# The last six layers of the first block in three passes, and where their weight splits stand in a step

## The chip, the cores and the metric

The kernel runs on one core of one Trainium2 chip. A core has engines that work side by side, each through a queue of its own in order: TensorE (PE, matrix products), VectorE (DVE, elementwise, reads PSUM), ScalarE (ACT, elementwise and copies, reads PSUM), GpSimd (POOL, elementwise on SBUF alone) and SyncE (SP, which here issues the DMA transfers). The metric is the device time of one execution in microseconds, as the median of several runs.

## The reference, cut to what matters

A linear-attention layer with decay (state `S x D x D` per head) makes `x` of 3072 tokens by 384. Then two feed-forward layers follow; the change is in the first one's weights and products:

```
def _moe_ref(x, w_in, w_out):          # 3072 x 384, 384 x 2048, 2048 x 384
    h = x @ w_in
    relu6 = np.clip(h + 3.0, 0.0, 6.0)
    g = h * relu6 / 6.0
    return (g @ w_out).astype(np.float32)
```

All of it is in 32-bit floating point.

## The kernel before, in words

The tokens are worked in six blocks `c` of 512 (128 steps of time for each of 4 batch entries). The hidden width 2048 is worked in 16 slices `f` of 128. In a *step* `n`, one pair (block, slice) is taken: `ff1` makes `hps`, the 128x512 product of the slice's input weights with the block's `x` in PSUM; ACT (line 462) and DVE (line 463, called *stt* below) apply the activation to it; and `ff2` adds the product of an earlier step's result with the slice's output weights onto `o`, two steps late (`while len(todo) > 2`). The first block is special: its slices 0 to 4 are done in halves of 256 tokens (steps 0 to 9), and from step 10 on it is whole slices, `n = f + 5`, up to step 20. The second block is steps 21 to 36, `n = f + 21`.

A product is done in one of two ways. *Full 32-bit*: three products of 128x128 by 128x512 (`emit_h_f32`, line 451, and `emit_out_f32`, line 457; each appears as two matmul records). *Three passes* (`emit_h`, line 445, and `emit_out`, line 474): both factors are split into a rounded high part and the low rest, and nine products are summed. Three passes need the parts of the weights, of `x` and of the activation's result `g`. In the first block the slices below `F32_F` (12) are done in full 32-bit, the rest, and all later blocks, in three passes.

The weights arrive as 64-bit numbers. For a slice `f` the class `Weight` does `load` (DMA into `raw`), `scale` (ACT, line 146), `bits` (DVE, lines 151 and 152; its result `x`, a staging tile with three buffers, is sent by a DMA into the slice's place in `wide_a` or `wide_b`, line 155), and later `parts`: ACT copies the high part (line 161) and DVE subtracts it from the value to leave the low part (line 162).

Between the products the attention runs as *jobs* `j` (one per batch entry and block), of which jobs 4 to 7 belong to the second block and 8 to 11 to the third. `plan(j, n)` puts a job over steps n to n+5: `scans` (DVE, line 280) and `bonus1` (POOL, lines 307, 308) in step n; `muls` (DVE, 303), `bonus2` (DVE, 312) and `decay` (POOL, 295 to 298) in n+1; `fill` (ACT, 338) in n+2, and in the middle of that step `pe_a` (PE, 357), `choose` (DVE, 363) and `copy_kt` (ACT, 350); in n+3 `pe_y` (PE, 393 and 399), `pe_u`, `copy_y` (ACT, 405, then seven transfers by SP that lay the result out) and `add_u` (DVE, 381); in n+5 `split` (ACT 421, POOL 422), which makes the parts of the next block's `x`. Jobs 7, 8, 9 and 10 begin at steps 15, 19, 23 and 27.

The order on every engine is written by hand. A step emits the list `before[n]`, then `ff1`, then `between[n]`, then `ff2` of two steps ago, then `behind[n]`; `pin()` ties each engine's instructions to this order:

```
        run(before[n])
...
        ff1(c, f, cols)
        run(between[n])
        while len(todo) > 2:
            ff2(*todo.pop(0))
        run(behind[n])
        pin()
```

A three-pass `ff1` also issues `emit_split` (ACT line 467, POOL line 468) right after the activation, so `ff1` of such a step is L462, stt, L467, L468. `x_parts` (lines 597 to 601) makes the parts of the first block's own `x`. The PSUM tile that `pe_y` writes is the one that `choose` of the same job has read, since their pool has one buffer; the tiles `hps` have two.

Of the kernel before, what the change touches and what calls it, by code (L numbers as in the profile page):

```python
# [9 lines left out]
F32 = mybir.dt.float32  # L10
# [3 lines left out]
AF = mybir.ActivationFunctionType  # L14
ALU = mybir.AluOpType
# [8 lines left out]
KT = DM // 128  # L24
F1 = 2048 // 128
# [4 lines left out]
WP = 4 * DM  # L30
NG = F2 // 3
LAGS = (5, 0, 0, 0, 0, 0)
F32_F = 12


@with_exitstack
def kernel(
# [15 lines left out]
    nc = tc.nc  # L53
# [23 lines left out]
    x0 = st_p.tile([128, KT, TOK], F32, tag="x0", name="x0", bufs=1)  # L77
# [53 lines left out]

    class Weight:
        def __init__(self, src):
            self.src, self.near = src, False

        def load(self):
            self.raw = st_p.tile([128, 2 * DM], U64, tag="raw", name="raw", bufs=3)
# [11 lines left out]
        def bits(self):  # L149
            x = st_p.tile([128, 2 * DM], U32, tag="x", name="x", bufs=3)  # L150
            nc.vector.tensor_scalar(x, self.words()[0], 29, None, ALU.logical_shift_right)
            nc.vector.scalar_tensor_tensor(
                out=x, in0=self.mag.bitcast(U32), scalar=3, in1=x, op0=ALU.logical_shift_left, op1=ALU.bitwise_or)
            self.x = x.bitcast(F32).rearrange("p (a n) -> p a n", a=2)
            nc.sync.dma_start(
                out=self.dst[:, :, 1, :].bitcast(U32), in_=x.rearrange("p (a n) -> p a n", a=2))
            if not self.near:
                self.x = self.dst[:, :, 1, :].bitcast(F32)
# [103 lines left out]
    xts = {0: xt_p.tile([128, KT, 2, TOK], F32R, tag="xt", name="xt")}  # L262
# [192 lines left out]
    def emit_out_f32(acc, slot, g, first, cols):  # L455
        for m in range(KT):
            nc.tensor.matmul(  # L457
                acc[m][:, cols], slot[:, m * 128:(m + 1) * 128], g,
                start=first, stop=True, skip_group_check=not first)
# [5 lines left out]
    def emit_split(a, n, p=None):  # L465
        g = (p or rg_p).tile([128, 2, n], F32R, tag="g", name="g")
        nc.scalar.activation(out=g[:, 0, :], in_=a, func=AF.Copy)  # L467
        nc.gpsimd.tensor_tensor(out=g[:, 1, :], in0=a, in1=g[:, 0, :].bitcast(F32), op=ALU.subtract)  # L468
        return g
# [9 lines left out]
    def new_acc():  # L479
        return [ps_o.tile([128, TOK], F32, tag=f"o{m}", name=f"o{m}") for m in range(KT)]  # L480
# [51 lines left out]
    wa = [Weight(wa_d[f]) for f in range(F1)]  # L532
# [9 lines left out]
    before, between, behind = ([[] for _ in steps] for _ in range(3))  # L542
# [38 lines left out]
        if f + 3 < F1:  # L581
            behind[n] += [wa[f + 3].load]
    for f in range(F1):
        before[f + 19 if f < F32_F else f + LAGS[0] - 1] += [wa[f].parts]
    behind[2] += [lambda: jobs[4].load("w", "rk", "rks", "v")]
    behind[4] += [lambda: jobs[5].load("w", "rk", "v")]

# [6 lines left out]
    for c in range(1, NC_):  # L594
        norm_plan(c, first[c], False)

    def x_parts():
        for k in range(KT):
            h = xts[0][:, k, 0, :]
            nc.scalar.activation(out=h, in_=x0[:, k, :], func=AF.Copy)  # L600
            nc.vector.tensor_tensor(out=xts[0][:, k, 1, :], in0=x0[:, k, :], in1=h.bitcast(F32), op=ALU.subtract)

    behind[F32_F + LAGS[0] - 2] += [x_parts]
    acc, norms, todo = None, {}, []


# [12 lines left out]
    def ff1(c, f, cols):  # L619
        n = cols.stop - cols.start  # L620
        ps = ps_h.tile([128, n], F32, tag="h", name="hps")
        if c == 0 and f < F32_F:
            if cols.start:
# [4 lines left out]
        else:  # L628
# [3 lines left out]
            g = emit_split(a, n)  # L632
        x = wa[f].x[:, 1] if c == 0 and f < F32_F else wpair[f][:, 1]
        todo.append((c, f, cols, g, x))

    def ff2(c, f, cols, g, x):
        nonlocal acc
        first, last = f == 0 and cols.start == 0, f == F1 - 1
        if first:
            acc = new_acc()  # L640
        if c == 0 and f < F32_F:
            emit_out_f32(acc, x, g, first, cols)
# [5 lines left out]
    def run(fs):  # L648
        for x in fs:
            x()  # L650
# [302 lines left out]
    for i in range(2):  # L953
        nc.sync.dma_start(
            out=uc[64 * i:64 * i + D, :, i], in_=u_d.rearrange("o (p i d) -> i d (o p)", p=NP, i=2)[i])
# [24 lines left out]
    for f in range(W1):  # L980
        wa[f].dst = wpair[f]
        wa[f].near = f < 2
    run((j0.scans, j0.pairs, j0.pe_bonus, j0.muls, j1.pairs, j0.fill, j0.pe_a, wa[0].scale, j1.pe_bonus, j1.fill))
    run((j1.scans, j0.choose, j1.muls, j1.pe_a, j0.pe_y0, wa[0].bits, wa[3].load, j1.choose, j1.pe_y0))
    run((wa[1].scale, wa[1].bits, wa[4].load, j2.pairs, j2.scans, j0.copy_y0, j1.copy_y0))
# [150 lines left out]
    for j in range(6 * NG + 1):  # L1136
        p, k = divmod(j, 2 * NG)
# [142 lines left out]
```

## Time and profile before

| | |
|---|---|
| median of 3 runs | 946.01 us (945.63 to 946.22) |
| the profiled execution | 945.5 us |
| its span in the profile | 943.7 us |
| PE busy | 928.6 us (98%) |
| DVE, ACT, POOL busy | 645.8, 475.8, 534.2 us |
| granted TensorE clock, mean | 0.998 |

The span is what the profiler saw from the first to the last instruction; 1.8 us lie around it. A row of a timeline gives the start, the time from start to end, the engine and line, what is written from what, and in brackets the idle time of the engine before it with what ended that. Merged instructions of one kind carry their count (x9).

### The profile page before, as it was taken

What the parts mean: (1) busy time and instruction counts of PE and PEld (TensorE: products, weight loads), DVE (VectorE), ACT (ScalarE), POOL (GpSimd) and SP (SyncE); (2) the same over time, 40 slices, a digit from 0 to 9 for tenths busy, and PEclk for the clock granted to TensorE, in tenths of its full rate; (3) what the DMA queues carried; (4) which work ended last, traced back from release to release, by engine and by line L of the source; (5) the groups of instructions that cost most, each with busy time, mean ns of one, the idle gap of its engine ahead of it and who ended that gap; (6) DMA issues with size and microseconds to landing.
All of it is one profiled execution on the core that took longest, in us unless ns stands there. A gap on an engine that the chain in (4) does not pass through costs nothing.

```text
span 943.7 us, 14286 instructions
## 1 busy us (share of the span) xinstructions
PE 928.6 (98%) x5085; PEld 734.6 (78%) x5085; DVE 645.8 (68%) x913; ACT 475.8 (50%) x946; POOL 534.2 (57%) x454
## 2 busy tenths in 40 slices
PE   5999999999999999999999999999999999999998
PEld 5875578778878887777888888887877778888886
DVE  7787767777778777776545477648888557554555
ACT  4554556546645554655454653446555444433331
POOL 0043255766756776674466677489466679335423
PEclk9999999999999999999999999999999999999999
DMA  9888532247546555652752387763699742644321
GB/s 347 299 300 286 201 135 84 85 144 251 190 132 202 176 168 154 229 179 59 239 197 97 130 309 265 272 242 156 220 376 335 262 162 89 245 167 153 149 79 67
DMA packets 63127, 184.77 MB, mean 196 GB/s; under 512 B 8912, under 2 KB 23248, under 8 KB 58448
## 3 DMA queue, kind: packets, MB, share of 16 engines
q1 hardware_dynamic: 63056, 183.87, 55.1%
q8 instruction: 40, 0.66, 0.3%
q14 instruction: 31, 0.25, 0.1%
HBM read 134.29 MB, written 39.32 MB: 184 GB/s over the span
## 4 chain that ended last, share of the span: by engine, by line
PE 90%; DVE 3%; DMA 2%; ACT 2%; SPq 1%; issue 1%; POOL 1%; POOLq 0%; DVEq 0%; ACTq 0%
PE o L474 17%; PE hps L445 16%; PE o L757 15%; PE pe L757 10%; PE pc L757 8%; PE pa L757 4%; PE hps L451 4%; PE o L457 3%; PE aps L357 3%; PE pb L757 3%; PE yps L399 2%; PE pd L757 1%; PE yps L393 1%; PE ktp L345 1%; PE yps L434 1%
## 5 line engine op out<-in xcount | busy, mean ns | idle before, releaser
L468 POOL TENSOR_TENSOR g<-a,g 128x512 fp32r<-128x512 f32 x84 | 116.0, 1381 | 146.6 <-ACT g L467 144.5
L463 DVE SCALAR_TENSOR_TENSOR a<-a,hps 128x512 f32<-128x512 f32 x84 | 57.2, 681 | 86.6 <-ACT a L462 85.1
L474 PE MATMUL o<-g,wide_b 128*128 128x512 f32 x441 | 113.3, 399 | 0.0
L445 PE MATMUL hps<-xt,wide_b 128*128 128x512 f32 x441 | 111.9, 398 | 0.0
L757 PE MATMUL o<-xt,wide_b 128*128 128x512 f32 x405 | 107.6, 395 | 0.0
L462 ACT ACTIVATE a<-hps,half 128x512 f32<-128x512 f32 x84 | 57.4, 684 | 92.5 <-PE hps L445 88.0
L445 PEld LDWEIGHTS hps<-xt,wide_b 128*128 128x128 f32 x441 | 82.7, 187 | 21.2 <-issue 1.2
L474 PEld LDWEIGHTS o<-g,wide_b 128*128 128x128 f32 x441 | 81.2, 188 | 19.5 <-issue 0.5
L467 ACT ACTIVATE g<-a 128x512 fp32r<-128x512 f32 x84 | 53.1, 632 | 79.4 <-DVE a L463 77.3
L757 PEld LDWEIGHTS o<-xt,wide_b 128*128 128x128 f32 x405 | 76.0, 188 | 18.2
L474 PE MATMUL o<-g,wide_a 128*128 128x512 f32 x315 | 78.7, 394 | 0.0
L280 DVE TENSOR_TENSOR_SCAN w<-w,dd 128x520 f32<-128x520 f32 x48 | 75.4, 1570 | 4.7 <-DMA w<-in_dram 3.1
L445 PE MATMUL hps<-xt,wide_a 128*128 128x512 f32 x315 | 77.6, 390 | 0.2 <-POOL xt L422 0.2
L445 PEld LDWEIGHTS hps<-xt,wide_a 128*128 128x128 f32 x315 | 59.0, 188 | 13.3 <-POOL xt L422 0.6
L474 PEld LDWEIGHTS o<-g,wide_a 128*128 128x128 f32 x315 | 58.2, 188 | 12.3 <-issue 0.2
L792 DVE TENSOR_TENSOR q<-pc,q 128x512 f32<-128x512 f32 x80 | 55.1, 688 | 17.6 <-PE pc L757 6.7
L338 ACT ACTIVATE a<-iperm,cb 128x128 f32<-128x128 f32 x192 | 58.5, 388 | 0.1
L858 POOL TENSOR_TENSOR q<-q,q 128x512 f32<-128x512 f32 x36 | 49.2, 1366 | 13.6 <-DVE q L792 13.4
L757 PE MATMUL o<-g,wide_b 128*128 128x512 f32 (+1 forms) x216 | 55.4, 390 | 0.0
L854 ACT ACTIVATE q<-q 128x512 f32<-128x512 f32 x40 | 25.3, 633 | 48.5 <-DVE q L792 48.5
L792 DVE TENSOR_TENSOR q<-pe,q 128x512 f32<-128x512 f32 x40 | 27.5, 688 | 32.1 <-PE pe L757 32.1
L307 POOL TENSOR_TENSOR rks<-rks 128x384 f32<-128x384 f32 x20 | 32.3, 1617 | 30.3 <-DMA rks<-in_dram 23.5
(206 smaller groups left out, 2005.2 us busy)
## 6 DMA issues: line engine op xcount, KB each, us to landing
wraw<-in_dram SPq DMA_DIRECT2D x36, 384.0 KB, 4.1
wide_b<-wo SPq DMA_DIRECT2D x12, 1152.0 KB, 8.3
w<-wd SPq DMA_DIRECT2D x10, 1280.0 KB, 6.1
wide_b<-wd SPq DMA_DIRECT2D x10, 1280.0 KB, 6.0
w<-in_dram SPq DMA_DIRECT2D x24, 520.0 KB, 3.9
rk<-in_dram SPq DMA_DIRECT2D x24, 512.0 KB, 5.0
raw<-in_dram SPq DMA_DIRECT2D x16, 768.0 KB, 7.5
rks<-in_dram SPq DMA_DIRECT2D x20, 384.0 KB, 5.7
```

The costliest lines, as they stand in the source:

```text
L280: nc.vector.tensor_tensor_scan(out=x, data0=x, data1=dd.rearrange("p a h j -> p (a h j)"), initial=0.0, op0=ALU.mult, op1=ALU.add)
L338: nc.scalar.activation(out=self.head(h), in_=iperm, func=AF.Copy, scale=self.cb[:, h, :])
L445: nc.tensor.matmul(ps, slot[:, l, k * 128:(k + 1) * 128], xt[:, k, r, :], start=(k == 0 and j == 0), stop=(k == KT - 1 and j == 2))
L451: nc.tensor.matmul(ps, slot[:, k * 128:(k + 1) * 128], xt[:, k, :], start=(k == 0), stop=(k == KT - 1))
L462: nc.scalar.activation(out=a, in_=ps, func=AF.Relu, scale=1.0 / 6.0, bias=half)
L463: nc.vector.scalar_tensor_tensor(out=a, in0=a, scalar=1.0, in1=ps, op0=ALU.min, op1=ALU.mult)
L467: nc.scalar.activation(out=g[:, 0, :], in_=a, func=AF.Copy)
L468: nc.gpsimd.tensor_tensor(out=g[:, 1, :], in0=a, in1=g[:, 0, :].bitcast(F32), op=ALU.subtract)
L474: nc.tensor.matmul(acc[m][:, cols], slot[:, l, m * 128:(m + 1) * 128], g[:, r, :], start=(first and j == 0), stop=(parts or last and j == ...
L757: nc.tensor.matmul(ps, lhs[:, l, :], rhs[:, r, :], start=first and j == 0, stop=True, skip_group_check=not (first and j == 0))
L792: nc.vector.tensor_tensor(out=out, in0=a, in1=b, op=op)
L858: eng.tensor_tensor(out=o, in0=src, in1=self.gate.o[i], op=ALU.mult)
```

## The change: what it does

`F32_F` becomes 10, so that slices 10 and 11 of the first block (steps 15 and 16) are done in three passes, like 12 to 15. For these six slices `bits` no longer sends its result by DMA (`stays`): `parts` reads the staging tile and writes both parts in place. The parts of slices 10 and 11 are made at the end of steps 13 and 14. Those of slices 12 to 15 stay in steps 16 to 19, and move from the end of the list `before` to its head. Those of slices 0 to 9, which the second block uses, stay in steps 19 to 28, and move from `before` to the end of `behind`. `x_parts` is cut in three, at the end of steps 6, 7 and 8 in place of step 15, with the subtraction on POOL in place of DVE.

```
-F32_F = 12
+F32_F = 10
...
-            self.src, self.near = src, False
+            self.src, self.near, self.stays = src, False, False
...
             self.x = x.bitcast(F32).rearrange("p (a n) -> p a n", a=2)
+            if self.stays:
+                return
             nc.sync.dma_start(
...
     for f in range(F1):
-        before[f + 19 if f < F32_F else f + LAGS[0] - 1] += [wa[f].parts]
+        if f < F32_F:
+            behind[f + 19] += [wa[f].parts]
+        else:
+            if f < 12:
+                behind[f + 3] += [wa[f].parts]
+            else:
+                before[f + 4].insert(0, wa[f].parts)
...
-    def x_parts():
-        for k in range(KT):
-            h = xts[0][:, k, 0, :]
-            nc.scalar.activation(out=h, in_=x0[:, k, :], func=AF.Copy)
-            nc.vector.tensor_tensor(out=xts[0][:, k, 1, :], in0=x0[:, k, :], in1=h.bitcast(F32), op=ALU.subtract)
-
-    behind[F32_F + LAGS[0] - 2] += [x_parts]
+    def x_parts(k):
+        h = xts[0][:, k, 0, :]
+        nc.scalar.activation(out=h, in_=x0[:, k, :], func=AF.Copy)
+        nc.gpsimd.tensor_tensor(out=xts[0][:, k, 1, :], in0=x0[:, k, :], in1=h.bitcast(F32), op=ALU.subtract)
+
+    for k in range(KT):
+        behind[6 + k] += [lambda k=k: x_parts(k)]
...
+    for f in range(F32_F, F1):
+        wa[f].stays = True
```

The queues of ACT and DVE in one step of the second block, say step 24 (slice 3, `muls` of job 9, `split` of job 8), are then, with `c` for the copy of a `parts` and `d` for its subtraction (`square` is a copy of the normalisation that follows a block):

```
before: ACT: L462, L467, split 8, square       DVE: muls 9, bonus2 9, d5, stt
        (c5 ahead of L462)
after:  ACT: L462, L467, split 8, c5, square   DVE: muls 9, bonus2 9, stt, d5
```

## Rows read from the trace of the kernel before

**Rows 1.** The page, busy time of PE: us, share of the span, instructions.

```profile
PE 928.6 (98%) x5085; PEld 734.6 (78%) x5085; DVE 645.8 (68%) x913; ACT 475.8 (50%) x946; POOL 534.2 (57%) x454
```

**Rows 2.** Waits of PE: line waited for: total us, times, longest.

```profile
PE yps L393 <- DVE a L363: 0.9, 1, 0.9
PE hps L445 <- POOL xt L422: 0.2, 1, 0.2
```

**Rows 3.** The chain that ended last: start, us, what.

```profile
101.53 2.58 PE hps L451 x6
104.11 2.58 PE o L457 x6
...
132.56 2.10 PE o L474 x9
```

**Rows 4.** Timeline of ACT and SP: the wait for a removed transfer, and its issue.

```profile
113.47 0.85 ACT L161 ACTIVATE wide_b<-wide_b 128x768 fp32r<-128x768 f32 x1 [1.62 <-DMA wide_b<-x]
...
114.43 0.65 SPq L155 DMA_DIRECT2D wide_b<-x  x1
```

**Rows 5.** Timeline of POOL, in steps 9, 18, 19 and 20.

```profile
60.58 1.30 POOL L307 TENSOR_TENSOR rks<-rks 128x384 f32<-128x384 f32 x1 [6.79 <-DVE a L363]
...
118.55 1.94 POOL L307 TENSOR_TENSOR rks<-rks 128x384 f32<-128x384 f32 x1
...
125.42 1.62 POOL L468 TENSOR_TENSOR g<-a,g 128x512 fp32r<-128x512 f32 x1 [3.03 <-ACT g L467]
127.00 1.73 POOL L422 TENSOR_TENSOR xt<-x,xt 128x384 fp32r<-128x384 f32 x1
```

**Rows 6.** Timeline of DVE, steps 14 to 19.

```profile
93.03 1.64 DVE L152 SCALAR_TENSOR_TENSOR x<-mag,x 128x768 uint32<-128x768 uint32 x1
...
96.23 1.24 DVE L280 TENSOR_TENSOR_SCAN w<-w,dd 128x520 f32<-128x520 f32 x1
...
100.34 1.89 DVE L601 TENSOR_TENSOR xt<-x,xt 128x512 fp32r<-128x512 f32 x3 [1.10 <-ACT xt L600]
102.15 1.28 DVE L303 TENSOR_TENSOR rk<-rk,w 128x512 f32<-128x512 f32 x2
...
103.82 0.95 DVE L162 TENSOR_TENSOR wide_b<-wide_b 128x768 fp32r<-128x768 f32 x1
...
117.72 1.96 DVE L280 TENSOR_TENSOR_SCAN w<-w,dd 128x520 f32<-128x520 f32 x1
...
124.00 0.67 DVE L463 SCALAR_TENSOR_TENSOR a<-a,hps 128x512 f32<-128x512 f32 x1
```

**Rows 7.** Timeline of ACT, steps 15 to 20.

```profile
104.73 0.91 ACT L146 ACTIVATE mag<-raw 128x768 f32<-128x768 f32 x1
105.54 2.44 ACT L338 ACTIVATE a<-iperm,cb 128x128 f32<-128x128 f32 x8
...
108.81 0.69 ACT L462 ACTIVATE a<-hps,half 128x512 f32<-128x512 f32 x1
...
117.14 0.58 ACT L405 ACTIVATE y<-yps 128x512 f32<-128x512 f32 x1
117.61 0.83 ACT L161 ACTIVATE wide_a<-wide_a 128x768 fp32r<-128x768 f32 x1
...
124.71 0.63 ACT L467 ACTIVATE g<-a 128x512 fp32r<-128x512 f32 x1 [1.86 <-DVE a L463]
125.25 0.51 ACT L421 ACTIVATE xt<-x 128x384 fp32r<-128x384 f32 x1
```

**Rows 8.** Timeline of PE and DVE: where jobs 9 and 10 meet.

```profile
155.74 1.36 DVE L363 COPY_PREDICATED a<-mask,aps 128x512 f32<-128x512 uint32 x2
...
157.25 0.67 PE L393 MATMUL yps<-rk,st 64*64 64x128 f32 x16
...
177.26 1.34 DVE L363 COPY_PREDICATED a<-mask,aps 128x512 f32<-128x512 uint32 x2
...
178.74 0.67 PE L393 MATMUL yps<-rk,st 64*64 64x128 f32 x16 [0.88 <-DVE a L363]
```

## The prediction

> **What bounds the kernel now.** I read the page first: PE is busy 98% of the span [rows 1]. The waits of PE come next. Past the start-up there are two of weight, 0.2 us for the split of `x` into the second block and 0.9 for a `choose`, both where blocks one and two meet [rows 2]. So PE sets the end, and a change pays what it takes off PE less what PE newly waits for. Then I read the timelines of the queues over the steps that the change touches; there ACT, DVE and POOL hand work to each other in a fixed order, with little to spare. Job 9's `choose` ends at 155.74 + 1.36 = 157.10 and PE's `pe_y` starts at 157.25; job 10's ends at 178.60, and there PE waits 0.88 [rows 8]. A slower ring of these three engines comes straight out as PE time.
>
> **PE's own work.** A product costs 2.58 in full 32-bit and 2.10 in three passes [rows 3]. Slices 10 and 11 have two each: 4 x 0.48 = **-1.92**. The Trainium skill ("FP8 and Floating Point Precision", section TensorE Precision Notes) says that true 32-bit takes four passes; beside three at 2.10 that would be 2.80 and -2.8 in all. The trace has 2.58, and I keep -1.92.
>
> **The transfers taken away.** Six of 393 KB (128 x 768 numbers of 4 bytes), with 0.65 us of SP's queue each [rows 4]. What is freed: the copy of slice 14 waited 1.62 for one [rows 4], and loads behind them on SP go out earlier. PE waited for none of it, so I count 0; a gain through it would have to show in a wait of PE, and rows 2 have only the two that I count below.
>
> **`x_parts` on POOL, steps 6 to 8.** DVE loses 1.89 at step 15 [rows 6]. POOL gets three subtractions of about 1.3 (as 60.58), into the 6.79 us in which it idled before that row [rows 5]; ACT gets three copies of some 0.6 in slack steps. They delay job 4's chain by about 0.6 and job 5's `bonus1` by about 1.4; PE is a step away from both. Between 0 and +0.5; I take 0.
>
> **Two habits of the queues.** An engine starts its next instruction about 0.1 before the shown end of the last (117.14 + 0.58 against 117.61), and another engine takes over some 0.03 after it (124.00 + 0.67 against 124.71) [rows 6, 7]. And DVE and POOL hold each other up: a scan takes 1.24 at 96.23 but 1.96 at 117.72, while POOL's L307 runs 1.94 beside it; the split L422 takes 1.73 at 127.00 beside a subtraction of DVE [rows 5, 6]. The Trainium skill ("SBUF — State Buffer", section SBUF: two separate sides) calls their shared port a lock held for the whole instruction; with no overlap at all of the two, my sum would come out about 0.5 us dearer. The rows, where the one held up finishes about 0.15 sooner than that, decide.
>
> **Steps 14 to 21: the first seam.** I wrote the new order of each queue as a timetable, with the rows' durations, and found this chain through DVE and ACT. From the end of `bits` 13 at 94.6 [rows 6]:
> - DVE: parts 11 is new there, 0.87; both scans of job 7 held up by `bonus1`, 3.8: step 15's stt at 99.2.
> - stt 0.7; ACT's L467, new, 0.54; `copy_y` 0.49; `scale` 0.81; copy of parts 12 0.85 [rows 7]: 102.6. DVE: subtraction 0.87, muls and reduce 1.67 (102.15 to 103.82) [rows 6]: stt of step 16 at 105.15.
> - 0.7; L467 0.54; `scale` 0.81; copy of parts 13, now ahead of `fill`, 0.74; `fill` 2.35; L462 0.7 [rows 7]: stt of step 17 at 111.0.
> - 0.6; `choose` 1.2; `bits` 15 held up by two POOL instructions, 2.8; parts 14 0.87: stt of step 18 at 116.5.
> - 0.7; L467 0.54; `copy_y` 0.49; copy of parts 15 0.86: 119.1. DVE: the subtraction held up, 1.7; scans 1.9, 0.1 and 1.2: stt of step 19 at 124.0.
>
> That is where it stood before (124.00 [rows 6]), although PE is now 1.92 ahead. After it ACT does L467, then the copy of parts 0, now in front of the split of job 7, which runs 126.0 to 126.5 and not at 125.25 [rows 7]. POOL's L422 begins at 126.6, meets the subtraction of parts 0 on DVE and takes 1.7 [rows 5]: it ends at 128.3. Before, it ended at 128.73 and PE waited 0.2 for it [rows 2, 5]; PE now wants it at 128.55 - 1.92 = 126.6. **A wait of 1.7 instead of 0.2.** PE keeps 0.45 of its 2.1.
>
> **Steps 19 to 28: parts at the end of the step.** Before, the copy of a parts was on ACT ahead of L462 and the subtraction on DVE ahead of the stt, mostly with its copy long done. Now the subtraction stands directly behind the stt, and its copy behind L467, which itself waits for that stt: DVE idles (0.68 + 0.03) + 0.54 + 0.86 - 0.60 = 1.5 us in every such step, with `scans` or `muls` of the next queued behind it. And as L467 also releases POOL's L468, the subtraction meets it and takes about 1.3.
>
> PE needs 178.74 - 0.88 - 157.25 = 20.6 us from one `pe_y` to the next [rows 8], eight products of 2.10 and 3.8 of attention, about half of it on each of the two steps that carry it. The ring needs:
> - Job 8. At 127.5 DVE has finished parts 0; muls, held up, and reduce 2.3; stt to L462 of step 21 with copy 1 and `fill` between, 5.05; stt and `choose` 1.9: done at 136.8. PE would be there at 157.25 - 20.6 - 0.45 = 136.2. **Wait 0.6.**
> - Job 9, counted from `pe_y` 8 at 136.8: attention and the block's last product 4.2; two ACT copies of the block's sum and copy 3, 1.9; subtraction and scans 3.3; stt to the subtraction of parts 4, 2.1; it, muls and reduce 3.2; stt, L467, split, copy 5, square, `fill`, L462 6.0; stt and `choose` 1.9. That is 22.6 against 20.6. **Wait 2.0.**
> - Job 10, from `choose` to `choose`: to step 26's stt 1.8; stt, L467, `copy_y`, copy 7 2.6; subtraction and scans, held up by `bonus1`, 5.0; stt to parts 8 2.1; it, muls (held up) and reduce 4.0; stt, L467, split, copy 9, `fill`, L462 5.5; stt and `choose` 1.9. That is 22.8. **Wait 2.2**, in place of 0.88.
>
> From step 29 on no parts are left (before: until step 30), the ring has slack again, and PE keeps the loss to the end.
>
> **Sum.** -1.92 - 0.2 - 0.88 + 1.7 + 0.6 + 2.0 + 2.2 = **+3.5**. The same timetable for the old order ends L422 at 128.4 (row 128.73) and job 10's `choose` at 177.55 (row 178.60): it falls short by up to 1.0 over these steps, and may do so here. I take +4.0: 945.5 + 4.0 = 949.5 for an execution like the profiled one. The median shown is 0.5 above that one, so **950.0**. Bounds: with no new wait at all -3.0 (943.0); with held-up instructions at their longest +5.2, and with the 0.5 of `x_parts` about +5.7 (951.7).
>
> **Rivals.**
> - *Faster: the ring keeps pace.* The parts leave the way of the stt, so that L467 and the split go earlier, and DVE's 1.5 us of idling falls into time that it had to spare (it is busy 645.8 of 943.7 [rows 1]). Its place is steps 19 to 28, its price the same -1.92 and up to -1.1 of old waits: 943.0 to 944.1 after adding 0.5 (with one wait of 1.4 left in job 9, which the timetable still has when no instruction holds up another, 944.4). It decides from where the seam is 1.7 shorter and the cycles 2 us shorter than I count. Against it: scans, muls and splits are plainly held up in rows 5 and 6, and `choose` had 0.15 to spare in job 9 and none in job 10 [rows 8].
> - *About the same: only the seam costs.* The wait of 1.7 comes, the job cycles hold at 20.6: -1.92 - 0.2 - 0.88 + 1.7 = -1.3, 944.7. Or one cycle pays and the sum is near 0. For it: half of each cycle (the steps with `fill` and `pe_y`) has room on DVE.
> - *The change does nothing for PE*, since three passes wait for parts 10 or 11: parts 11 end at 95.4 and are wanted at 101.53 - 0.48 [rows 3], and parts 10 have as much of a step. No chance of weight.
>
> **How the numbers follow.** I give the forecast 0.70, the ring that keeps pace 0.17, the seam alone or one cycle 0.13. 0.2% is 1.9 us, about what a measurement here can tell from no change: faster is under 944.1, slower over 947.9. So faster 0.17, same 0.13, slower 0.70. The forecast's own range is 948.0 to 952.3; the range that reaches to the others is 943.8 to 952.3.
>
> **What would show it.** Three-pass products in steps 15 and 16 at 2.1 each. A wait of PE for L422 of 1 us or more at step 21; then waits of `pe_y` for `choose` in jobs 8, 9 and 10, of which the last two are near 2. DVE idle by about 1.5 in front of L162 in steps 19 to 28, ended by ACT's L161. If L162 stands there with little idle, or PE's waits past step 21 stay under 1 us in sum, the prediction is wrong, and on the fast side.

## The result, and the profile after

| | before | after |
|---|---|---|
| median of 6 runs, us | 946.12 (945.24 to 946.90) | 951.52 (949.34 to 953.98) |
| ratio, 95% interval | | 1.006 (1.0049 to 1.0070) |
| profiled execution, us | 945.5 | 951.95 |
| its span, us | 943.7 | 950.2 |

The change makes the kernel slower by 5.4 us. It was forecast slower, at 950.0 in a range of 943.8 to 952.3. Below `bits` the code of the kernel after stands two lines lower and, from L593 on, eight: L464, L465, L469, L470 are the activation, the stt and the two parts of `emit_split`, L163 and L164 the two halves of a `parts`, L365 is `choose`, L395 the first product of `pe_y`, L424 POOL's split.

Busy time of PE on the page of the kernel after, in us, with its share of the span and its instructions:

```profile
PE 929.4 (98%) x5097; PEld 738.4 (78%) x5097; DVE 645.6 (68%) x910; ACT 476.8 (50%) x948; POOL 543.6 (57%) x459
```

Twelve more PE instructions are there (four products of nine for six), and PE is busier by only 0.8 us than in [rows 1], so 5.7 of the 6.5 us by which the span grew are waiting. Waits of PE in the kernel after (total us, times, longest):

```profile
PE cps L328 <- DVE rp L322: 8.8, 1, 8.8
PE yps L395 <- DVE a L365: 3.6, 3, 2.2
...
PE hps L447 <- POOL xt L424: 1.2, 1, 1.2
PE pe L765 <- DMA w<-wd: 1.1, 1, 1.1
...
PE hps L447 <- DVE wide_a L164: 0.3, 1, 0.3
```

Beside [rows 2], the split wait went from 0.2 to 1.2, the `choose` waits from one of 0.9 to three, and two lines are new: the one for a subtraction of a `parts`, and one for a DMA. Now PE's timeline, where each of them stands:

```profile
88.42 2.74 PE L453 MATMUL hps<-x,wide_b 128*128 128x512 f32 x6
...
127.59 0.39 PE L447 MATMUL hps<-xt,wide_a 128*128 128x512 f32 x1
129.15 2.14 PE L447 MATMUL hps<-xt,wide_a 128*128 128x512 f32 x8 [1.17 <-POOL xt L424]
...
137.74 0.67 PE L395 MATMUL yps<-rk,st 64*64 64x128 f32 x16 [0.60 <-DVE a L365]
...
151.03 1.89 PE L447 MATMUL hps<-xt,wide_a 128*128 128x512 f32 x7 [0.26 <-DVE wide_a L164]
...
160.91 0.67 PE L395 MATMUL yps<-rk,st 64*64 64x128 f32 x16 [2.22 <-DVE a L365]
161.51 1.52 PE L401 MATMUL yps<-a,v 128*64 128x128 f32 x16
...
183.89 0.67 PE L395 MATMUL yps<-rk,st 64*64 64x128 f32 x16 [0.80 <-DVE a L365]
...
707.02 0.94 PE L765 MATMUL pe<-wide_b,w 128*128 128x512 f32 x3 [1.09 <-DMA w<-wd]
```

Three of these rows are anchors: the product of step 14, the first of step 21, and job 10's `pe_y`. In the kernel before the last began at 178.74 [rows 8], the others here:

```profile
87.12 2.74 PE L451 MATMUL hps<-x,wide_b 128*128 128x512 f32 x6
...
128.20 0.39 PE L445 MATMUL hps<-xt,wide_a 128*128 128x512 f32 x1
```

After, the three stand at 88.42, 127.59 and 183.89: +1.30, -0.61, +5.15. So PE gains 1.91 between the first two, and loses 5.76 between the others. The +1.30 arose at start-up, ahead of everything that the change touches (PE's first wait, for `rp`, is 8.8 here and was 7.9 before); among the kernels below the start-up differs from one profiled execution to the next by as much. What the change did by step 31 is **+3.85**.

The row of L401 at 161.51 takes 1.52 where the same row (L399, at 157.85) took 1.09 before. Windows of 3 us there (busy time of each engine, then PE's granted clock, the DMA share and GB/s):

```profile
158.00:161.00 3.00, 0.78 (x8) 0.35 (x10) 1.93 (x3) 2.25 (x5) 0.74 (x1) 1.00 0.00 0
161.00:164.00 3.00, 3.00 (x49) 2.74 (x50) 1.75 (x3) 2.25 (x5) 2.10 (x3) 0.67 0.00 0
164.00:167.00 3.00, 3.00 (x11) 2.41 (x12) 2.08 (x4) 1.62 (x3) 2.55 (x2) 0.76 0.13 38
167.00:170.00 3.00, 3.00 (x15) 2.48 (x14) 2.93 (x3) 0.69 (x1) 2.92 (x3) 1.00 0.10 27
```

PE was busy for 0.78 of the first 3 us, and behind that wait the granted clock fell for a while to the lower of its two levels, 1.2 GHz. The two windows lose 3 x 0.33 + 3 x 0.24 = 1.7 us. This fall belongs to the execution that was profiled: it lists a mean granted clock of 0.996, two of the six timed ones 1.000 (949.34 and 951.08 us), and one such fall alone would take that mean to 0.998 (1.7 us of 950). Against the kernel before, the waits sum to 1.17 - 0.19 + 0.60 + 0.26 + 2.22 + 0.80 - 0.88 = 3.98; with -1.92 for the products and 1.7 for the clock that is 3.76, of the 3.85 seen.

What feeds those waits is seen on DVE (the bracket is idle time ahead, and what ended it):

```profile
126.82 1.43 DVE L164 TENSOR_TENSOR wide_a<-wide_a 128x768 fp32r<-128x768 f32 x1 [1.43 <-ACT wide_a L163]
...
132.73 1.41 DVE L164 TENSOR_TENSOR wide_a<-wide_a 128x768 fp32r<-128x768 f32 x1 [1.43 <-ACT wide_a L163]
...
149.56 1.41 DVE L164 TENSOR_TENSOR wide_a<-wide_a 128x768 fp32r<-128x768 f32 x1 [1.44 <-ACT wide_a L163]
...
155.40 1.02 DVE L164 TENSOR_TENSOR wide_a<-wide_a 128x768 fp32r<-128x768 f32 x1 [1.85 <-ACT wide_a L163]
...
158.83 0.69 DVE L465 SCALAR_TENSOR_TENSOR a<-a,hps 128x512 f32<-128x512 f32 x1 [2.41 <-ACT a L464]
159.44 1.33 DVE L365 COPY_PREDICATED a<-mask,aps 128x512 f32<-128x512 uint32 x2
```

Ten subtractions stand at the end of a step. Each begins after an idle that the copy of the same `parts` ends: 1.37 to 1.85 in seven of them, 0.66 to 0.88 in three. Four run 1.41 to 1.43 where one took 0.95 before [rows 6]; they begin while POOL's L470 of the same step still runs (from 126.13 for 1.30, beside the first). The other six take 0.96 to 1.17. At 158.83 the last two rows show job 9's end of it: the stt waits for ACT's L464, which stands behind `fill` and the copy, and `choose` behind it ends at 160.77, when PE has already been waiting.

### The profile page after: what moved, and what is told of

Its sections match the earlier page's. It is cut to its first block, busy times and chain, and to the rows that moved or that the text cites. A ratio compares the mean times of both kernels' runs of the same rounds, so it can differ in the third digit from the quotient of the medians.

```text
span 950.2 us, 14303 instructions
## 1 busy us (share of the span) xinstructions
PE 929.4 (98%) x5097; PEld 738.4 (78%) x5097; DVE 645.6 (68%) x910; ACT 476.8 (50%) x948; POOL 543.6 (57%) x459
## 4 chain that ended last, share of the span: by engine, by line
PE 83%; DVE 8%; ACT 4%; DMA 3%; issue 3%; SPq 0%; ACTq 0%; DVEq 0%
PE o L476 17%; PE hps L447 15%; PE o L765 13%; PE pe L765 9%; PE pc L765 8%; PE pa L765 4%; PE hps L453 3%; PE pb L765 3%; PE aps L359 2%; PE o L459 2%; PE yps L401 2%; DVE w L282 1%; PE pd L765 1%; PE yps L395 1%; PE yps L436 1%
## 5 line engine op out<-in xcount | busy, mean ns | idle before, releaser
L470 POOL TENSOR_TENSOR g<-a,g 128x512 fp32r<-128x512 f32 x86 | 116.9, 1359 | 144.7 <-ACT g L469 144.6
L465 DVE SCALAR_TENSOR_TENSOR a<-a,hps 128x512 f32<-128x512 f32 x86 | 58.6, 681 | 93.1 <-ACT a L464 91.5
L476 PE MATMUL o<-g,wide_b 128*128 128x512 f32 x459 | 118.0, 400 | 0.0
L447 PE MATMUL hps<-xt,wide_b 128*128 128x512 f32 x459 | 116.5, 397 | 0.0
L464 ACT ACTIVATE a<-hps,half 128x512 f32<-128x512 f32 x86 | 58.8, 684 | 96.6 <-PE hps L447 93.2
L447 PEld LDWEIGHTS hps<-xt,wide_b 128*128 128x128 f32 x459 | 86.1, 187 | 22.0 <-issue 1.0
L476 PEld LDWEIGHTS o<-g,wide_b 128*128 128x128 f32 x459 | 84.4, 188 | 20.2 <-issue 0.5
L469 ACT ACTIVATE g<-a 128x512 fp32r<-128x512 f32 x86 | 54.4, 633 | 89.3 <-DVE a L465 87.2
L765 PEld LDWEIGHTS o<-g,wide_b 128*128 128x128 f32 x216 | 40.0, 188 | 9.4
```

What stands on the lines that cost most here:

```text
L447: nc.tensor.matmul(ps, slot[:, l, k * 128:(k + 1) * 128], xt[:, k, r, :], start=(k == 0 and j == 0), stop=(k == KT - 1 and j == 2))
L464: nc.scalar.activation(out=a, in_=ps, func=AF.Relu, scale=1.0 / 6.0, bias=half)
L465: nc.vector.scalar_tensor_tensor(out=a, in0=a, scalar=1.0, in1=ps, op0=ALU.min, op1=ALU.mult)
L476: nc.tensor.matmul(acc[m][:, cols], slot[:, l, m * 128:(m + 1) * 128], g[:, r, :], start=(first and j == 0), stop=(parts or last and j == ...
L765: nc.tensor.matmul(ps, lhs[:, l, :], rhs[:, r, :], start=first and j == 0, stop=True, skip_group_check=not (first and j == 0))
```

## The experiments

All times are medians in us; ratios are to the kernel before, timed beside each on the same chip.

**One half alone, and the other half alone.** e1 is the kernel before with nothing but the `parts` of slices 0 to 11 at the end of their steps; e2 the kernel after with those of 0 to 9 back ahead.

```
e1 (on before):  before[f + 19] -> behind[f + 19]   for f < F32_F
e2 (on after):   behind[f + 19] -> before[f + 19]   for f < F32_F
```

> The kernel before, with one edit: the parts of slices 0 to 11 stand at the end of steps 19 to 30 and no longer ahead of the product. My theory (DVE idles behind the activation until ACT has done L467 and the copy): no wait at step 21, since parts 0 then leave the way there; waits of pe_y for choose of about 2 us in jobs 9 and 10; +3.9 us against the kernel before, some 1 to 2 more if the clock falls after such a wait as in the changed kernel. Rival (the extra work of the two new three-pass slices on ACT and POOL fills the queues): no change, within 1 us.

> The changed kernel, with the parts of slices 0 to 9 put back ahead of the product in steps 19 to 28; all else as changed. My theory: the waits for choose go, the wait for the split of job 7 at step 21 grows from 1.2 to about 3 us, since parts 15 and parts 0 both stand in front of it again; +0.8 us against the kernel before (-1 to +2.5 with a fall of the clock after that wait). Rival (three passes in steps 15 and 16 are the cause): as slow as the changed kernel, +5.

e1: 949.26, ratio 1.0044 (1.0024 to 1.0063). e2: 947.44, 1.0014 (0.9994 to 1.0035). In e1 PE waits for the `choose` of jobs 9 and 10:

```profile
159.97 0.67 PE L393 MATMUL yps<-rk,st 64*64 64x128 f32 x16 [2.23 <-DVE a L363]
182.94 0.67 PE L393 MATMUL yps<-rk,st 64*64 64x128 f32 x16 [1.88 <-DVE a L363]
```

In e2 no `choose` wait is left, and the seam costs more. Its timeline, and the windows around:

```profile
129.87 3.48 PE L447 MATMUL hps<-xt,wide_a 128*128 128x512 f32 x8 [2.44 <-POOL xt L424]
```

```profile
125.00:130.00 5.00, 2.31 (x10) 1.34 (x9) 4.37 (x7) 2.76 (x5) 3.43 (x3) 1.00 0.96 338
130.00:135.00 5.00, 5.00 (x29) 3.70 (x29) 1.67 (x3) 4.06 (x12) 1.87 (x3) 0.66 0.68 243
```

So the waits of 2 us in jobs 9 and 10 come from the `parts` at the end of the steps, the wait at step 21 does not, and the seam alone cancels what the products give. In e2 too the clock falls behind the wait (0.66 for 5 us: 1.7), in the execution profiled.

**A copy ahead, a subtraction behind.** The subtraction at the end stands behind a copy that waits for the stt. In e3 the copy goes back ahead of the product and only the subtraction stays at the end. e4 also puts the late slices 12 to 15 back at the end of `before`.

```
e3 (on after):  before[f + 19] += [wa[f].high];  behind[f + 19] += [wa[f].low]
e4 (on e3):     before[f + 4].insert(0, wa[f].parts) -> before[f + 4] += [wa[f].parts]
```

> The changed kernel, with only ACT's copy of slices 0 to 9 put back ahead of the product; DVE's subtraction stays at the end of the step. My theory: the copy is long done when DVE comes to the subtraction, so the 1.4 us of idling goes; waits for choose under 0.6 us each, the wait of about 1.2 to 1.7 us at step 21 stays; 0 us against the kernel before (-1 to +1.5). Rival (it is the late subtraction itself, or POOL meeting it, that is dear): +4 or more, like the changed kernel.

> As the kernel with the copy first, and the parts of slices 12 to 15 back at the end of the list ahead of the product, as in the kernel before. My theory: parts 13 no longer stand in front of fill and parts 15 no longer in front of the scans, so the chain through steps 16 to 19 is shorter and no wait is left at step 21: -2.4 us against the kernel before (three passes 1.92, the old waits 0.2 and 0.9). Rival (the head of the list is the better place, as parts 15 are wanted at step 20): a wait for parts 15 at step 20, and slower than the kernel with the copy first.

e3: 945.55, 0.9998 (0.9985 to 1.0012). e4: 944.45, 0.9989 (0.9975 to 1.0003). So it is the late copy that is dear, and the rival of e3 falls: with the subtraction alone at the end, the time is that of the kernel before. In e3 one `choose` wait of 1.09 is left, more than was expected, and the split wait of 1.49 stands; in e4 the first is 1.08 and the split wait is gone (no row of it), so that one comes from the `parts` at the head of steps 16 to 19. e4 has job 10's `pe_y` at 176.94, 1.8 ahead of the kernel before, but gained 0.8 only: at 700 us PE waits 1.2 for a DMA that it did not wait for before. That is taken up below.

**One tile of ten.** By the timetable the wait of job 9 comes from slice 4 alone.

```
e5 (on after):  (before if f == 4 else behind)[f + 19] += [wa[f].parts]
```

> The kernel after, with the parts of slice 4 alone (step 23) put back ahead of the activation, as in the kernel before; the parts of slices 0 to 3 and 5 to 9 stay at the end of their steps. Theory: the 2.22 us wait of PE for the choose of job 9 comes from this one tile, because its copy at the end of step 23 holds up the fill of step 25 and its subtraction the choose; a timetable from the rows' durations lets the wait of job 9 go from 2.1 to 0 and keeps those of step 21, job 8 and job 10. The granted clock of TensorE fell to 0.67 and 0.76 in the 6 us after that wait in the kernel after, worth some 1.7 us; if the wait causes the fall, it goes too, and the first product of step 31 comes 3.5 to 4 us earlier than in the kernel after relative to step 14: some 947.5 us where the kernel after has 951.5. Rival, the clock fell on its own account: the fall stays, and the gain is 2.2 alone. Rival, the time goes to all end-of-step parts alike: one tile in ten takes a tenth of it back, under 0.5 us.

950.15, ratio 1.0056 (1.0037 to 1.0076), where the kernel after has 1.0060: not 3.5 to 4 us faster, but 1.4 by the medians and less by the ratios. Its timeline of PE at jobs 9 and 10:

```profile
158.28 0.67 PE L395 MATMUL yps<-rk,st 64*64 64x128 f32 x16 [0.49 <-DVE a L365]
...
181.24 0.67 PE L395 MATMUL yps<-rk,st 64*64 64x128 f32 x16 [1.88 <-DVE a L365]
```

The tile is the right one: job 9's wait falls from 2.22 to 0.49, and the clock stays at 1.00 in 158 to 167 (e6 below shows that it can stay there behind the longer wait too). But job 10's wait rises from 0.80 to 1.88, what it is in e1 as well. While PE ran at the lower clock in the kernel after, the queues caught up with it: of the 1.7 that the clock took, the next wait gave 1.1 back. From job 7's `pe_y` (113.94) to job 10's, e5 takes 67.30 us; the kernel after, from 114.92, 68.97.

**The two parts that I counted at nothing.** e6 has the subtractions of `x_parts` on DVE again, e7 the six transfers kept.

```
e6 (on after):  nc.gpsimd.tensor_tensor(out=xts[0]... -> nc.vector.tensor_tensor(out=xts[0]...
e7 (on after):  wa[f].stays = True -> wa[f].stays = False
```

> The kernel after, with the subtraction of the first block's x parts at the ends of steps 6 to 8 on DVE again in place of POOL. Theory: these three operations lie where both engines have idle time and PE waits for neither, so the engine is free: within 0.1% of the kernel after, and the same waits of PE. Rival: on POOL they hold DVE up at the port that the two share and push the activations late, so that DVE would be 1 to 2 us better. Rival: on DVE they push bits or choose of job 4 late, 1 to 2 us worse.

> The kernel after, with the six transfers of slices 10 to 15 kept (the parts read what the transfer brought, as in the kernel before). Theory: the transfers cost SP some 0.65 us each and land before the parts of slices 11 to 15 need them, or delay only a copy with slack behind it; no wait of PE hangs on them except perhaps at the first three-pass product of step 15, whose parts come at the end of step 13, up to 0.5 us. Within 0.1% of the kernel after. Rival: that the staging tiles stay without a transfer is what the change gains, and the kernel is 1 to 3 us slower with them.

e6: 951.60, 1.0072 (1.0057 to 1.0087), the kernel after within what can be told. e7: 953.44, 1.0089 (1.0074 to 1.0104), 1.8 over e6 on the same chip, where the intervals just overlap, and clear of the 1.0060 of the kernel after (up to 1.0070). So the expectation for e7 fell. ACT and PE of e7, and a window of it:

```profile
116.36 0.85 ACT L163 ACTIVATE wide_b<-wide_b 128x768 fp32r<-128x768 f32 x1 [2.84 <-DMA wide_b<-x]
117.12 0.67 ACT L464 ACTIVATE a<-hps,half 128x512 f32<-128x512 f32 x1
```

```profile
128.00 0.49 PE L447 MATMUL hps<-xt,wide_a 128*128 128x512 f32 x1 [0.67 <-ACT xt L423]
129.87 3.15 PE L447 MATMUL hps<-xt,wide_a 128*128 128x512 f32 x8 [1.38 <-POOL xt L424]
```

```profile
130.00:135.00 5.00, 5.00 (x29) 3.78 (x29) 3.43 (x5) 2.94 (x8) 2.66 (x4) 0.66 0.55 171
```

The copy waits 2.84 for a transfer and holds up the activation of step 18 right behind it. At the seam PE then waits 0.67 + 1.38 where it waits 1.17 in the kernel after, and the clock falls there (0.66 for 5 us: 1.7). In the kernel before nothing hung on the copy's 1.62 [rows 4]: the activation behind it (L462 at 115.16) waits another 0.84 for PE. So the transfers are no longer free. How much of the 1.8 is theirs is not settled: from job 7's to job 10's `pe_y` e7 takes 70.74 us and e6 68.97, but e6 has its own fall of the clock right behind that, and to job 11's `pe_y` the two take 91.94 and 91.76.

e6 shows where the clock can go. Its waits are those of the kernel after (2.19 for job 9), yet no fall follows that one; it follows the next (windows as above):

```profile
182.45 1.00 PE L395 MATMUL yps<-rk,st 64*64 64x128 f32 x16 [1.88 <-DVE a L365]
```

```profile
162.00:165.00 3.00, 3.00 (x15) 2.47 (x14) 1.31 (x4) 2.18 (x4) 2.13 (x3) 1.00 0.11 30
182.00:185.00 3.00, 2.55 (x32) 2.25 (x34) 0.99 (x2) 1.41 (x3) 1.83 (x2) 0.61 0.02 5
185.00:188.00 3.00, 3.00 (x28) 2.59 (x25) 1.73 (x3) 1.88 (x2) 2.48 (x3) 0.82 0.08 22
```

**Three passes alone.** e8 is the kernel before with `F32_F = 10` and nothing else.

> The kernel before with F32_F = 10 alone: two more slices of the first block in three passes, their parts in the list ahead of the activation two steps later than their turn would allow, and the parts of x at the end of step 13; no other part of the change. Theory: the four products give 1.9 us back, and waits for late parts at the head of steps 15 to 20 and at the seam take it, by the timetable some 2.9 us, so +1.0 (-0.5 to +2.5) against the kernel before, with waits of PE hps for the low parts (DVE) of slices 10 to 15 in the chain and none of PE yps above 1 us. Rival, the products give their 1.9 and the queues absorb the rest: 944 us.

948.60, 1.0041 (1.0024 to 1.0057): +3.2, over the +2.5 that was allowed for. Its timeline of PE at step 20, and the window there:

```profile
126.40 2.41 PE L445 MATMUL hps<-xt,wide_b 128*128 128x512 f32 x7 [2.85 <-DVE wide_b L162]
```

```profile
125.00:130.00 5.00, 3.60 (x11) 2.85 (x12) 4.77 (x6) 2.52 (x4) 2.84 (x3) 0.76 0.66 229
```

The wait for the low part of slice 15 alone is over the 1.9 of the products; the fall of the clock behind it and 1.1 at 700 us were not expected. So the products do not pay without the rest of the change. Ahead of that low part, ACT's copy of slice 14 waits for its transfer:

```profile
116.87 0.85 ACT L161 ACTIVATE wide_b<-wide_b 128x768 fp32r<-128x768 f32 x1 [3.03 <-DMA wide_b<-x]
```

The activation of step 18 follows at 117.62, and on DVE the subtraction of `parts` 0 (122.98, 1.69) still stands in front of the one of slice 15. It is not the head order that takes this wait away: e4, and e10 below, have the late slices at the end of `before` as e8 has, and no wait for a `parts` of theirs. They have neither that transfer nor the subtraction of `parts` 0 ahead, and they have `x_parts` and slices 10 and 11 earlier; which of these counts was not tested.

**The wait at 700 us.** At 677 us the activations of each kernel so far still have the distance to the kernel before that they had at 217, within 0.1 us; then all of them with `F32_F = 10` wait 0.9 to 2.6 at one row, for `w<-wd`. That load is issued late because SP waits for another, `wide_b<-wo`, issued at about 680. In the kernel before and e1 it lands after 6.7 us; with `F32_F = 10` after 8.5 to 9.7. The one thing found in the DMA views that goes with it is a packet of instructions on queue q14. DMA view of the kernel after, in the 2 us behind the issue of that load (packets, MB, share; KB, us to landing):

```profile
q1 hardware_dynamic: 237, 0.53, 97.7%
q14 instruction: 1, 0.01, 1.3%
...
wide_b<-wo SPq DMA_DIRECT2D x1, 1152.0 KB, 8.7
```

In the kernel before and e1 the packet comes 9.5 to 9.8 us behind the issue; in the others within a microsecond. The DMA engines are full there (a share of 0.9 to 1.02 from 680 to 700, in the kernels before and after). To tell the packet from the rest of `F32_F = 10`, e9 shifts the code of ACT and POOL by two idle instructions each, on the kernel before:

```
def fillers(k):
    nc.scalar.activation(out=pads[0], in_=half, func=AF.Copy)      # 128x1
    nc.gpsimd.memset(pads[1], 0.0)                                 # 128x1
e9 (on before):  at the ends of steps 30 and 31
e10 (on after):  (before if f in (3, 4, 7, 8) else behind)[f + 19] += [wa[f].parts]
                 late slices 12 to 15: as in e4
e11 (on e10):    fillers at the ends of steps 30 to 35
```

> The kernel before, with two tiny activations (128x1) and two tiny memsets of POOL added at the ends of steps 30 and 31, where both engines have over 1 us of idle time; nothing else is changed and none of its results is used. In all eight kernels with F32_F = 10 profiled so far, the transfer of wide_b from wo at about 680 us takes 8.6 to 8.8 us from issue to landing where the two kernels with F32_F = 12 show 6.7, a packet of instructions (q14) is fetched in the half microsecond or so behind its issue where the two others have it 9.5 us later, and PE then waits 0.9 to 2.6 us for the weights w of wd at about 700 to 707 us where the two others wait for nothing there. F32_F = 10 gives ACT and POOL two instructions more each. Theory: the two instructions move the fetch ahead into the stretch of full DMA engines, so this kernel, with the products of the kernel before, shows the fetch at about +0, a landing of 8.7 and a wait of 0.9 to 1.2 at about 700: some 946.3 to 946.7 us against 945.4 (+0.1%). Rival, the wait comes from the times at which the transfers of this stretch are asked for, or from something else that goes with F32_F = 10: fetch, landing (6.7) and time stay as in the kernel before, to 0.05%.

> The kernel after, with the parts of slices 3, 4, 7 and 8 (steps 22, 23, 26, 27) back ahead of the activation and those of the late slices 12 to 15 at the end of the list before again; slices 0 to 2, 5, 6 and 9 stay at the end of their steps. Theory: only the parts that share a step with the fill or the choose of a job, or lie in the step ahead of them, cost PE a wait at the end of a step, and only those at the head of steps 16 to 19 cost the seam; a timetable from the rows' durations leaves no wait over 0.3 us from step 14 to 31 and puts yps of job 10 some 2.3 us ahead of the kernel before. The stage at about 700 takes 1 to 1.2 back, so 944 to 944.9 against 945.4. Rival, the copies of the three-pass slices hold PE up elsewhere: 946 or more.

> As e10_four_of_ten, with six tiny activations and six tiny memsets of POOL at the ends of steps 30 to 35. Theory, as for e9_fillers: they move the fetch of the instructions several microseconds ahead of the issue of the load of wo, its landing goes back towards 6.7 us, and the wait for w from wd at about 700 us goes: some 943.0 to 943.7. Rival, the fetch has nothing to do with it: same as e10_four_of_ten to 0.05%, with a landing of 8.6 to 8.8 and the wait.

e9: 948.54, 1.0029 (1.0017 to 1.0041). e10: 943.98, 0.9984 (0.9970 to 0.9998). e11: 943.81, 0.9979 (0.9968 to 0.9991). The two idle instructions bring the wait into the kernel before. Its DMA view in the 2 us behind the issue, and its wait:

```profile
q14 instruction: 1, 0.01, 1.1%
...
wide_b<-wo SPq DMA_DIRECT2D x1, 1152.0 KB, 9.0
```

```profile
PE pe L765 <- DMA w<-wd: 1.6, 1, 1.6
```

In e11 the packet is fetched 1.4 us ahead of the issue, the load lands after 6.8, and the wait (1.4 in e10) is gone. So idle instructions bring the late landing in and take it away, and each time it goes with the place of the fetch. But e9 lost 3.0 and not 1, and e11 gained 0.2 on e10 and not 1.4. For e9 the trace has two more terms: 1.6 of start-up, which is that one execution's (it took 950.12), and a drift; the drift is in e11 too. The activations that stand at 195.93 and 677.39 in the kernel before stand at 197.54 and 680.02 in e9: 1.0 later, with no wait listed. The distance grows little by little, slowly at first (1.67 at 300 us, 1.80 at 400, 2.06 at 500, 2.49 at 600). Both have two new tiles of 4 bytes, and no other kernel drifts. e12 takes the tiles away and keeps the fillers:

```
e12 (on e10):  nc.scalar.activation(out=spare, in_=eps, func=AF.Copy)     # spare, st: there before
               nc.gpsimd.memset(st_all[0][:, 0:1], 0.0)
```

> As e11_four_of_ten_fillers (the kernel e10_four_of_ten with six tiny activations and six tiny memsets of POOL at the ends of steps 30 to 35), but the fillers write a tile that is there already and a margin of the state tile, in place of two new tiles of 4 bytes each. In e9 and e11, the two kernels with the new tiles, the activations of one step lag more and more behind those of their partners without fillers, by 1.0 us from 200 to 680 us, evenly; in none of the eight other kernels do they lag by over 0.1 there. Theory 1, the new tiles move all others by 8 bytes and that costs TensorE a little on every product: this kernel shows no such drift. Theory 2, the fetch of instructions: the landing of the load of wo stays at 6.7 to 6.8 us, and PE does not wait for w from wd at about 700 us. Both together: e10 less its wait of 1.4, 942.3 to 942.9 us against 945.5, and a spread of the runs nearer to that of the kernel before. Rival to 1, the fillers' own instructions or the chip cause the drift: it stays, some 943.8. Rival to 2: the wait of 1 to 2 us comes back.

**941.96, ratio 0.9956 (0.9941 to 0.9971)**: 3.6 faster than the kernel before and some 9.5 than the kernel after. No drift, no wait at 700, and the runs lie within 0.5 us but one, where those of e10 spread over 5.0. All waits of PE in e12 over 0.3:

```profile
PE cps L328 <- DVE rp L322: 7.9, 1, 7.9
PE hps L453 <- DMA wide_a<-x: 1.7, 1, 1.7
PE aps L359 <- issue: 1.5, 1, 1.5
PE aps L359 <- DVE rk L305: 0.7, 1, 0.7
PE hps L453 <- ACT x L441: 0.6, 1, 0.6
PE yps L395 <- DVE a L365: 0.4, 1, 0.4
```

All but the last stand ahead of step 6. Between steps 14 and 31 only 0.4 is left of 5.05.

## Why the prediction was right, point by point

- **Products, -1.92.** Right: -1.91 from step 14 to 21. The -2.8 of the four passes did not come; it had put every pass at the same price, and the rows can't tell the number of passes from their price (2.58/12 = 0.215 us each if they are four, 2.10/9 = 0.233 in three).
- **Transfers, 0.** Wrong as it was meant: kept, they would cost something, 1.8 by the medians of e7 and e6, of which the traces up to job 11 show 0.2. The step that failed is the inference that what PE did not wait for before it would not wait for later. The result doesn't contain that cost, since they are gone, so the sum is untouched.
- **`x_parts` on POOL, 0.** Right as far as can be told (e6, ratio 1.0072 against 1.0060 of the kernel after).
- **Seam, 1.7.** 1.17, over-sized by 0.5. Of the two causes that were named one holds: the chain of the late slices, which leaves the stt of step 19 where it stood although PE is ahead. In e10, without the head order, that stt begins at 122.94 where it begins at 124.73 in the kernel after, and the wait is gone. The other, the copy of `parts` 0 ahead of the split and its subtraction beside POOL's split, makes no wait by itself: both are in e10 too, with the split at 1.72 (1.71 in the kernel after), and e2 and e3, with that copy back ahead, still wait 2.44 and 1.49.
- **Jobs 8, 9, 10: 0.6, 2.0, 2.2.** 0.60, 2.22, 0.80. Not counted was 0.26 for a subtraction of a `parts` at 151. The mechanism is shown by e1 and e3, for slice 4 by e5, and for slices 3, 4, 7 and 8 together by e10. The idle of about 1.5 does not come in every step, as was written, but in seven of ten, and the slowed subtraction in four. Job 10's wait was over-sized, 1.88 where the clock had not fallen (e1, e5, e6), and 0.80 behind the fall.
- **What the sum lacked, and luck.** Two terms of some size: the fall of the granted clock behind a wait, 1.7, of which job 10's wait gave 1.1 back; and 1.4 at 700 us (ACT's rows are 5.16 late at 677 and 6.53 at 706), which goes with the fetch of instructions. The sum's own terms, put at +3.5, come to -1.91 - 0.19 - 0.88 + 1.17 + 0.60 + 2.22 + 0.80 = +1.8 in this execution; the clock's 1.7 and the 0.26 take that near the +3.85 seen up to step 31, and the wait far downstream makes it 5.2, against +5.4 by the medians. So the direction and the mechanism of the ring were right, and it is luck that +4.0 lies so near: seam and job 10 were over-sized by 1.9 together, and two costs that were not forecast stand in for them.
- **The rivals.** The ring that keeps pace is refuted by e1, the seam alone by e1 too; e2 shows the seam alone as about the same, as that rival had it, once the ring is taken away.

## What to carry to other kernels

Before an instruction goes to the end of a step, look for a job in the step behind it that waits on the same engine: of the ten tiles moved here, the four ahead of the `scans` and `muls` of jobs 9 and 10 cost PE the waits of those jobs, and with only the other six moved 0.4 is left in all (e10). Price a wait of the bounding engine above its length where the clock may fall behind it, and below it where the next wait will shrink. When a gain ahead is gone far behind, compare the distance of the two traces row by row: here it stayed constant for 480 us and was lost in one row, to a transfer that the code had not touched.

## What the runs showed of the hardware

- **Instruction fetches have a place.** An 0.01 MB packet of instructions in a stretch of full DMA engines goes with a landing of 8.5 to 9.7 us for a 1152 KB load, in ten kernels; elsewhere (1.4 ahead or 9.5 and more behind the issue) it is 6.7 to 6.9, in four. The Trainium skill ("Runtime: NRT & Kernel Launch", section Instruction fetch mechanics) says that an engine fetches its next block of code by a DMA of its own, at a cost mostly hidden. The packets on q14 agree with the first; as to the cost, a wait of PE of 0.9 to 2.6 us went with them here. Whether the packet was ACT's or POOL's, and how so small a one costs the load 2 us, stays open.
- **The clock does not fall behind every wait.** It fell after 2.22 (kernel after), 2.44 (e2), 0.67 + 1.38 (e7) and 2.85 (e8), and after 1.88 in e6; not after 2.23 and 1.88 in e1, 2.19 in e6, 1.88 in e5. Executions of one kernel differ too: their mean granted clocks are 0.995 to 1.000 in the kernel after and in e2. What decides was not found.
- **Eight bytes of SBUF.** Two tiles of 4 bytes more, ahead of the others, and PE lost 1.0 us in some 480 (e9, e11). That it is the address of the tiles is argued from e12, which has the fillers without the tiles and no drift; no single product was shown to be slower.
